# A new written order for the steps of both halves of a fused attention, gated MLP and rational MLP kernel

## The chip, the cores and the metric

The kernel runs on one core of one Trainium2 chip. The metric is the device time in microseconds (us) of one execution. Engines are named as in the profile: PE is TensorE (PEld its weight loads), DVE is VectorE, ACT is ScalarE, POOL is GpSimd, SP is SyncE, whose queue issues nearly all DMA transfers.

## What is computed

The reference, cut to what matters (8 batches, 8 heads, 576 rows of 64; 4608 tokens of 512):

```python
p_packed = sm_attn(p, k, v)            # 32 packed queries per head read the whole sequence
out = sm_attn(q, p_packed, p_packed)   # the sequence reads the 32 packed rows
x = out as (4608, 512)
xn = x / rms(x) * rms_g
x = (silu(xn @ w_gate) * (xn @ w_val)) @ w_out         # d_ff 1536
h = x @ w_in                                           # d_ff 2048
g = (a0 + a1 h + a2 h^2 + a3 h^3) / (1 + |b0||h| + |b1| h^2 + 1e-6)
return g @ w_out2
```

## The kernel before

Products that need float32 accuracy are done as three float16 products: each operand is split into a high part (written by ACT) and a low part (the difference, written by DVE or POOL). The weights arrive as 64-bit numbers and are decoded on DVE by three integer operations (lines 131, 135, 137).

**First half** (batches 0 to 7). For each batch attention gives normalised tokens (`an`, lines 655 to 919), and the packed values times the gate and value weights give `mt` (lines 415 to 447), so that the gated MLP needs only short products. The MLP is cut into two column ranges of 256 and 320 tokens and 12 blocks of 128 features. For each there are the steps G (gate product, line 1340), A (tanh on ACT, 1351), D (DVE, 1355), V (value product, 1340), E (DVE, 1358), Y and Z (high and low part of `y`, ACT 1362 and POOL 1367); the steps O and o are the second product (line 1393), P and S evict and store the result (`x2e`, 1372 and 1385). G, V, O and the attention's products take turns in five PSUM banks of the pool `ps_m`: a product can start only when the step that reads the bank's last content (D, E, P) is done. Meanwhile the weights of the third MLP are decoded, recombined and split (steps that begin with u, lines 1500 to 1534, POOL and ACT) and stored.

**Second half** (nine token blocks of 512, j = 0 to 8). The product with `w_in` is done with seven products instead of eight (a Strassen-like scheme). The operands `xo` of a block are made from the loaded block `xf` by the steps x: `s3` to `s6` sums on DVE (line 1636), `h0` to `h6` high parts on ACT (1626, 1630), `l0` to `l6` seven low parts on POOL (1633). A group g (block j, one of four column groups) has the products m1 to m7 (line 1685, `h`), the evictions k1 to k3 on ACT (`su`, 1693; products 6, 7 and 4 add to the bank that these read, so each of them must wait for the eviction ahead of it), sums a1 to a3 on DVE (1696), and for each of four result tiles the rational function: A (two ACT operations, 1726 and 1728), w and W (POOL, 1731 and 1736), t and u (DVE, 1739 and 1742), l and x (Ln and Exp on ACT, 1745 and 1748), q, e, g (DVE, 1751, 1754, 1757), h and i (high and low part of the result, ACT 1761 and POOL 1765). Then come the products o with `w_out2` (line 1789), the eviction f and the store F (1805, 1807, 1811). Products A, B and C of a group take turns in three PSUM banks of the pool `ps_h`; step g frees one.

**What sets the order.** Every step is a small function in the dictionary `steps`, and one long text, `ORDER` (line 947), names all 6932 of them in the order in which their instructions are put into the engines' queues. Each engine works its own queue strictly in that order and waits, where an operand is not there yet, with all that is queued behind. The text has four segments, parted by `|`, between which memory pools change: 3422 steps (the first half up to batch 7's MLP), 256 (the rest of batch 7, with the loads of the second half's weights), 82 (the first group of the second half) and 3172 (the rest). In the last segment the order repeats itself: the stretch from the first product of a block to the first product of the next has, from block 3 to block 6, the same 362 names in the same order, shifted by a block (block 2 nearly so, block 7 but for its end); blocks 0 and 1 are ordered freely.

```python
seg = [x.split() for x in ORDER.split("|")]
for nm in seg[0]:
    steps[nm]()
```

Of the kernel before, what the change touches and what calls it, by code (L numbers as in the profile page):

```python
# [9 lines left out]
F32 = mybir.dt.float32  # L10
# [27 lines left out]
def attention_pack_glu_rational_kernel(  # L38
# [641 lines left out]
    def attention(b):  # L680
# [1206 lines left out]
```

## Time and profile before

| what | value |
|---|---|
| time, median of 3 runs | 1498.63 us (1497.63 to 1499.5) |
| the profiled execution's own time | 1500.81 us |
| its span, first to last instruction | 1499.0 us |
| mean granted TensorE clock | 0.991 |
| PE busy | 1441.7 us, 96% of the span |
| DVE, ACT, POOL busy | 1197.8, 999.9, 858.8 us |
| DMA | 149.55 MB, mean 100 GB/s |

The span is what lies between the first and the last instruction; the profiled execution took 1.8 us more than its span and 2.2 us more than the median of the runs. Busy time is the sum of what an engine executed; a matmul's end is modelled, so PE's idle time is read as a lower bound of what it loses.

### The profile page before, as it was taken

The numbers are of one execution on the slowest core, as the hardware profiler recorded it, in microseconds if no ns is written. First come the engines' busy times: TensorE is split into PE (matmuls) and PEld (weight loads), VectorE is DVE, ScalarE is ACT, GpSimd is POOL, SyncE is SP. The second block draws the span as 40 slices with busy tenths as digits, with TensorE's granted clock in tenths as the row PEclk, the third lists the DMA queues.
The fourth block names the chain that finished last, engine by engine and source line by source line (L and its number), as shares of the span: only waits on it lengthen the run. The fifth ranks groups of instructions, "written<-read, shape, count | busy, mean of one in ns | idle before, by whom it ended". The sixth has DMA issues, their size and how long they took to land.

```text
span 1499.0 us, 31046 instructions
## 1 busy us (share of the span) xinstructions
PE 1441.7 (96%) x11940; PEld 1014.9 (68%) x11940; DVE 1197.8 (80%) x2160; ACT 999.9 (67%) x2042; POOL 858.8 (57%) x898
## 2 busy tenths in 40 slices
PE   7879999998999999999999999999999999999998
PEld 5557776867777677777877665666666666666665
DVE  5899867799887979987358897888787888787776
ACT  3555766776666676676357876777776767676665
POOL 1133142545557465353447877768686868686665
PEclk8899999999999999999999999999999999999999
DMA  9776663556868676795621001101010101000000
GB/s 269 196 223 134 127 148 69 108 138 145 190 158 203 153 193 165 199 193 131 255 94 34 29 15 43 57 1 57 1 57 1 57 1 57 1 15 15 15 15 29
DMA packets 212581, 149.55 MB, mean 100 GB/s; under 512 B 151888, under 2 KB 186704, under 8 KB 211280
## 3 DMA queue, kind: packets, MB, share of 16 engines
q1 hardware_dynamic: 212336, 147.57, 38.0%
q8 instruction: 93, 1.52, 0.4%
q14 instruction: 56, 0.46, 0.1%
q0 software_dynamic: 96, 0.01, 0.0%
HBM read 85.46 MB, written 30.41 MB: 77 GB/s over the span
## 4 chain that ended last, share of the span: by engine, by line
PE 67%; DVE 13%; POOL 9%; ACT 6%; issue 3%; DMA 2%; SPq 0%; ACTq 0%; DVEq 0%; POOLq 0%
PE o L1789 17%; PE h L1685 15%; PE o L1393 14%; PE gv L1340 13%; POOL xo L1633 2%; POOL w L1736 2%; POOL g L1765 2%; POOL w L1731 1%; PE xo L891 1%; DVE raw L135 1%; PE mm L415 1%; DVE t L1358 1%; PE mm L417 1%; PE pk L811 1%; DVE t L1355 1%
## 5 line engine op out<-in xcount | busy, mean ns | idle before, releaser
L1789 PE MATMUL o<-w2o,g 128*128 128x512 f16 x1728 | 410.6, 379 | 0.0
L1685 PE MATMUL h<-xo,w2t 128*128 128x256 f16 x3024 | 368.6, 272 | 9.8 <-ACT su L1693 9.6
L1685 PEld LDWEIGHTS <-w2t 128*128 128x128 f16 x3024 | 295.4, 98 | 97.9 <-issue 17.6
L1340 PE MATMUL gv<-an,mt 128*128 128x256 f16 (+1 forms) x2304 | 306.8, 286 | 14.7 <-DVE t L1355 6.4
L1393 PE MATMUL o<-y,wo 128*128 128x256 f16 (+1 forms) x2304 | 303.0, 287 | 6.6 <-DVE t L1355 3.3
L1367 POOL TENSOR_TENSOR y<-t,y 128x256 f16<-128x256 f32 (+1 forms) x192 | 161.9, 852 | 253.3 <-ACT y L1362 233.8
L1340 PEld LDWEIGHTS <-mt 128*128 128x128 f16 x2304 | 222.8, 98 | 79.3 <-issue 21.3
L1789 PEld LDWEIGHTS <-g 128*128 128x128 f16 x1728 | 169.0, 98 | 154.6 <-POOL g L1765 0.2
L1393 PEld LDWEIGHTS <-wo 128*128 128x128 f16 x2304 | 223.5, 98 | 73.9 <-issue 16.2
L1765 POOL TENSOR_TENSOR g<-t,g 128x512 f16<-128x512 f32 x140 | 167.8, 1199 | 115.4 <-ACT g L1761 115.4
L1736 POOL TENSOR_TENSOR w<-w,ah 128x512 f32<-128x512 f32 x140 | 178.7, 1278 | 10.8
L1731 POOL TENSOR_SCALAR w<-ah,cf 128x512 f32<-128x512 f32 x140 | 109.0, 779 | 58.1 <-ACT ah L1726 58.1
L1761 ACT ACTIVATE g<-t 128x512 f16<-128x512 f32 x140 | 88.5, 634 | 62.0 <-DVE t L1757 62.0
L1355 DVE SCALAR_TENSOR_TENSOR t<-t,gv 128x256 f32<-128x256 f32 (+1 forms) x192 | 84.5, 446 | 52.4 <-ACT t L1351 51.4
L1362 ACT ACTIVATE y<-t 128x256 f16<-128x256 f32 (+1 forms) x192 | 81.8, 437 | 62.6 <-DVE t L1358 61.4
L1351 ACT ACTIVATE t<-gv 128x256 f32<-128x256 f32 (+1 forms) x192 | 76.6, 405 | 70.4 <-PE gv L1340 51.1
L1745 ACT ACTIVATE h<-w,one 128x512 f32<-128x512 f32 x105 | 72.9, 695 | 69.7 <-POOL w L1736 51.6
L1751 DVE SCALAR_TENSOR_TENSOR t<-t,cf,h 128x512 f32<-128x512 f32 x105 | 78.1, 743 | 48.1 <-ACT h L1748 46.9
L1358 DVE SCALAR_TENSOR_TENSOR t<-t,gv 128x256 f32<-128x256 f32 (+1 forms) x192 | 84.5, 448 | 39.1 <-PE gv L1340 33.1
L1728 ACT ACTIVATE t<-h,cf 128x512 f32<-128x512 f32 x105 | 82.3, 783 | 0.8 <-POOL g L1765 0.8
L1742 DVE SCALAR_TENSOR_TENSOR t<-t,cf,h 128x512 f32<-128x512 f32 x105 | 78.4, 747 | 3.4
L1726 ACT ACTIVATE ah<-h 128x512 f32<-128x512 f32 x108 | 64.5, 597 | 22.1 <-PE h L1685 13.9
(223 smaller groups left out, 2161.0 us busy)
## 6 DMA issues: line engine op xcount, KB each, us to landing
raw<-in_moe_w_out_dram SPq DMA_DIRECT2D x28, 512.0 KB, 4.2
xf<-x2s SPq DMA_DIRECT2D x9, 1024.0 KB, 4.8
raw<-in_k_dram SPq DMA_DIRECT2D x16, 512.0 KB, 5.1
raw<-in_q_dram SPq DMA_DIRECT2D x16, 512.0 KB, 4.5
raw<-in_v_dram SPq DMA_DIRECT2D x16, 512.0 KB, 5.2
raw<-in_moe_w_in_dram SPq DMA_DIRECT2D x16, 512.0 KB, 4.6
out_dram<-osb SPq DMA_DIRECT2D x32, 256.0 KB, 2.4
w2t<-raw SPq DMA_DIRECT2D x28, 256.0 KB, 2.6
```

Of the source, the lines that this page charges most:

```text
L1340: nc.tensor.matmul(out=ps, lhsT=mt[b, nm, c // 4, g][:, l, cs], rhs=an[b][:, 2 * r_ + g, cols], start=(n == 0), stop=(n == 5))
L1355: stt(out=t, in0=t, scalar=1.0, in1=ps_g, op0=ALU.add, op1=ALU.mult)
L1358: stt(out=t, in0=t, scalar=S_Y / (2.0 * (S_AN * S_M) ** 2), in1=ps_v, op0=ALU.mult, op1=ALU.mult)
L1367: nc.gpsimd.tensor_tensor(out=y[:, 1], in0=t, in1=y[:, 0], op=ALU.subtract)
L1393: nc.tensor.matmul(out=ps, lhsT=wo1[c][:, l, d * 128:(d + 1) * 128], rhs=ys[b, h, c][:, r_, :], start=(c == 0 and n == 0), stop=(c == NF1 ...
L1685: nc.tensor.matmul(out=st[x][:, W2 * e:W2 * e + W2], lhsT=w[:, l, 128 * cs:128 * cs + 128], rhs=xs[j][:, OPERAND[p], r_, kc], start=(first ...
L1728: act(out=st["t", n], in_=st[x], func=AF.Identity, scale=cf[:, 0:1], bias=cf[:, 7:8])
L1731: nc.gpsimd.tensor_scalar(out=st["w", n], in0=st["ah", n], scalar1=cf[:, 6:7], scalar2=cf[:, 5:6], op0=ALU.mult, op1=ALU.add)
L1736: nc.gpsimd.tensor_tensor(out=st["w", n], in0=st["w", n], in1=st["ah", n], op=ALU.mult)
L1761: act(out=g[:, 0], in_=st["t", n], func=AF.Copy)
L1765: nc.gpsimd.tensor_tensor(out=g[:, 1], in0=st["t", n], in1=g[:, 0], op=ALU.subtract)
L1789: nc.tensor.matmul(out=po[k], lhsT=g[:, l, 256 * i + 128 * u:256 * i + 128 * u + 128], rhs=w2t["o", 0, c][:, r_, :], start=(done[k] == 0), ...
```

## The change

Only the text `ORDER` is new. Each of its four segments names the same steps as before, each once; the second and the third segment are word for word the same (only their line breaks differ), the first and the last are in another order throughout. No instruction is added, removed or resized. The text is one line longer, so that every line below it has a number higher by one.

```diff
     ORDER = (
-        "wl9 wb9 0pl 0pf 0ph L1 0kf10 0kf12 0kg10 0kg12 wl7 wc9 wd9 0kf11 0kg11 0am1 cc L0 0kf00 wb7 0kg00 0kf01 "
+        "L1 0kf10 wl4 wb4 wc4 wd4 0pl 0kf12 0pf 0ph 0kf11 0kg10 wl2 0kg12 wb2 wc2 wd2 cd 0kg11 0am1 L0 0kf00 wl3 "
...
```

In the last segment the repeated pattern is gone: the order differs from block to block throughout.

**Second half, POOL, while the operands of block 4 are made.** `xo` rows are the low parts of the block's operands (from `xf`, the loaded block, or `sx`, a sum of its quarters), `w` rows the two steps of the rational function's denominator, `g` rows the low parts of its result. Before:

```order
L1633 TENSOR_TENSOR xo<-xf,xo 128x512
L1765 TENSOR_TENSOR g<-t,g 128x512
L1633 TENSOR_TENSOR xo<-sx,xo 128x512
L1731 TENSOR_SCALAR w<-ah,cf 128x512
L1736 TENSOR_TENSOR w<-w,ah 128x512
L1765 TENSOR_TENSOR g<-t,g 128x512
L1633 TENSOR_TENSOR xo<-xf,xo 128x512 x2
L1731 TENSOR_SCALAR w<-ah,cf 128x512
L1736 TENSOR_TENSOR w<-w,ah 128x512
L1765 TENSOR_TENSOR g<-t,g 128x512
L1633 TENSOR_TENSOR xo<-xf,xo 128x512
L1633 TENSOR_TENSOR xo<-sx,xo 128x512
```

Now, from the first of this block's `xo` rows on:

```order
L1634 TENSOR_TENSOR xo<-sx,xo 128x512
L1766 TENSOR_TENSOR g<-t,g 128x512
L1634 TENSOR_TENSOR xo<-xf,xo 128x512
L1732 TENSOR_SCALAR w<-ah,cf 128x512
L1766 TENSOR_TENSOR g<-t,g 128x512
L1732 TENSOR_SCALAR w<-ah,cf 128x512
L1737 TENSOR_TENSOR w<-w,ah 128x512 x2
L1732 TENSOR_SCALAR w<-ah,cf 128x512
L1737 TENSOR_TENSOR w<-w,ah 128x512
L1766 TENSOR_TENSOR g<-t,g 128x512
L1732 TENSOR_SCALAR w<-ah,cf 128x512
L1737 TENSOR_TENSOR w<-w,ah 128x512
```

All seven `xo` operations of a block stood within 13 rows of POOL's queue (six of them are shown); now they stand within 33 rows for block 4, two in the first twelve. For block 8, the last, they stand within 18 rows.

**Opening, SP's queue from the program's first transfer on.** `raw` and `rawt` are k or q of batch 0, `praw` is p, numbered `raw_` tiles are weights. Before:

```order
L148 DMA raw_178<-in_moe_w_gate_dram 128x512
L293 DMA praw<-in_p_dram 32x8x64
L251 DMA raw<-in_k_dram 128x4x256
L255 DMA rawt<-in_k_dram 64x4x64
L148 DMA raw_211<-in_moe_w_val_dram 128x512
L251 DMA raw<-in_k_dram 128x4x256
```

Now:

```order
L251 DMA raw<-in_k_dram 128x4x256
L255 DMA rawt<-in_k_dram 64x4x64
L148 DMA raw_191<-in_moe_w_val_dram 128x512
L293 DMA praw<-in_p_dram 32x8x64
L148 DMA raw_221<-in_moe_w_gate_dram 128x512
L251 DMA raw<-in_k_dram 128x4x256
```

The first load of k is the first transfer now and was the third; p is the fourth and was the second; the second load of k is the sixth in both. PE's queue begins with the transposes of k (line 490) now, and began with those of p (line 473).

## Rows read from the trace of the kernel before

**Rows 1.** The page's parts 1 and 2: PE's busy time, and its granted clock.

```profile
PE 1441.7 (96%) x11940; PEld 1014.9 (68%) x11940; DVE 1197.8 (80%) x2160; ACT 999.9 (67%) x2042; POOL 858.8 (57%) x898
PEclk8899999999999999999999999999999999999999
```

**Rows 2.** Windows by stage: length; busy PE, PEld, DVE, ACT, POOL; PEclk, DMA share, GB/s.

```profile
0.00:112.00 112.00, 86.96 (x702) 58.84 (x703) 88.50 (x197) 54.63 (x132) 21.05 (x35) 0.89 0.80 229
112.00:340.00 228.00, 225.12 (x2288) 167.96 (x2286) 182.51 (x408) 150.15 (x362) 86.55 (x120) 1.00 0.56 123
340.00:600.00 260.00, 245.22 (x2551) 187.34 (x2539) 220.47 (x436) 173.06 (x418) 151.97 (x167) 1.00 0.72 171
600.00:768.00 168.00, 167.30 (x1593) 129.41 (x1592) 111.57 (x243) 94.36 (x231) 69.66 (x86) 1.00 0.70 191
799.00:922.00 123.00, 122.95 (x821) 79.84 (x820) 109.33 (x159) 92.18 (x158) 99.63 (x91) 1.00 0.08 27
922.00:1443.00 521.00, 511.35 (x3437) 335.80 (x3435) 424.89 (x630) 377.01 (x646) 379.88 (x353) 1.00 0.07 25
1443.00:1499.00 56.00, 51.85 (x322) 31.15 (x319) 39.83 (x61) 34.44 (x58) 33.03 (x31) 0.98 0.05 20
```

**Rows 3.** Waits of PE from 922 to 1443: us in total, times, longest.

```profile
PE h L1685 <- ACT su L1693: 9.6, 12, 1.3
```

**Rows 4.** Timeline of PE around 1025: start, us, [idle before <- releaser].

```profile
1025.26 1.47 PE L1685 MATMUL h<-xo,w2t 128*128 128x256 f16 x12 [1.29 <-ACT su L1693]
1031.04 1.47 PE L1685 MATMUL h<-xo,w2t 128*128 128x256 f16 x12 [0.41 <-ACT su L1693]
```

**Rows 5.** Timeline of POOL just before that.

```profile
1022.12 1.16 POOL L1633 TENSOR_TENSOR xo<-xf,xo 128x512 f16<-128x512 f32 x1
1023.24 1.16 POOL L1633 TENSOR_TENSOR xo<-sx,xo 128x512 f16<-128x512 f32 x1
1024.38 0.77 POOL L1731 TENSOR_SCALAR w<-ah,cf 128x512 f32<-128x512 f32 x1
```

**Rows 6.** Timeline of ACT in the same stretch.

```profile
1021.08 0.69 ACT L1745 ACTIVATE hd<-w,one 128x512 f32<-128x512 f32 x1 [1.09 <-POOL w L1736]
1024.58 0.62 ACT L1693 ACTIVATE su<-h 128x512 f32<-128x512 f32 x1
```

**Rows 7.** Waits of weight loads from 799 to 1443.

```profile
PEld L1685 <- DVE t L1757: 1.3, 3, 0.5
```

**Rows 8.** Timeline of SP, then of PE, in the first 8 us.

```profile
0.72 0.39 SPq L148 DMA_DIRECT2D raw<-in_moe_w_gate_dram  x1
1.64 0.45 SPq L251 DMA_DIRECT2D raw<-in_k_dram  x1
...
5.32 0.60 PE L473 MATMUL first<-squares,praw 32*128 32x32 f32 x4 [5.32 <-DMA praw<-in_p_dram]
6.93 1.33 PE L490 MATMUL first<-squares,raw 128*64 128x128 f32 x10 [1.01 <-DMA raw<-in_k_dram]
```

**Rows 9.** Two windows of the opening, columns as in rows 2.

```profile
12.15:29.20 17.05, 13.60 (x189) 10.39 (x186) 14.29 (x39) 9.26 (x25) 0.00 (x0) 1.00 1.04 320
29.20:49.70 20.50, 18.93 (x106) 13.55 (x113) 14.42 (x30) 5.96 (x14) 0.00 (x0) 0.50 0.75 220
```

**Rows 10.** Waits of PE from 340 to 600, the largest.

```profile
PE gv L1340 <- DVE t L1355: 5.5, 5, 1.9
```

**Rows 11.** Timeline of DVE and of POOL from 348 to 353.

```profile
348.68 1.48 DVE L749 SCALAR_TENSOR_TENSOR v<-rawt,v 64x256 f16<-64x256 f32 x1
351.17 1.36 DVE L749 SCALAR_TENSOR_TENSOR x16in<-raw,x16in 128x256 f16<-128x256 f32 x1
...
348.41 1.48 POOL L1534 TENSOR_TENSOR raw<-raw,raw 128x512 f32<-128x512 f32 x1 [0.27 <-ACT raw L1500]
```

**Rows 12.** Instructions of two lines: duration ns min/median/max, first and last start us, forms.

```profile
L749 DVE SCALAR_TENSOR_TENSOR v<-rawt,v x14: 403/409/1480, 130.5 to 662.4; 64x256 f16<-64x256 f32 x14
L1355 DVE SCALAR_TENSOR_TENSOR t<-t,gv x192: 400/424/489, 57.3 to 767.0; 128x256 f32<-128x256 f32 x96, 128x320 f32<-128x320 f32 x96
```

761 rows, old and new, of the table ORDER are left out of this document.

## The prediction

> **What bounds the kernel now.** I read the page first, for which engine is full; then the windows by stage, for where that engine loses time; then the waits of each stage and the timeline around one of them. PE is busy for 1441.7 of 1499.0 us [rows 1]. Since no instruction is added or removed, an order can win only what PE does not use, 57.3 us, and what it does at the lower clock; both must be looked for by stage. The windows [rows 2] are to be read as length minus PE busy. The first 112 us lose 25.0 us; 112 to 340 loses 2.9; 340 to 600 loses 14.8; 600 to 768 loses 0.7. In the second half, 799 to 922 loses 0.05 us in 123, 922 to 1443 loses 9.65 in 521, and the end loses 4.1. So there are three places: the opening, the middle of the first half, and the repeated part of the second half.
>
> The repeated part has one cause. All of PE's waits there are products that wait for an eviction by ACT: 12 waits, 9.6 us [rows 3], two for each of six blocks, of some 1.3 and 0.4 us [rows 4]. The timeline shows why. POOL makes the seven low parts of the next block's operands, 1.16 us each and so 8.1 us, in one run of 13 queue rows [rows 5]; with them it has no pause and falls behind with the denominators (w, then W). ACT works strictly in order, and its Ln step stands there waiting for W, 1.09 us at 1021 [rows 6]. The eviction is queued behind that Ln and starts at 1024.58; PE's product follows at 1025.26 [rows 4]. The stretch from 799 to 922, whose order is not the repeated one, has the same mix of work and loses nothing.
>
> **The change, part by part.** The sum is made against the profiled execution, 1500.81 us; the median of the runs is 2.2 us lower, and the result is carried to it at the end.
>
> *The second half.* The seven low parts of block 4 now lie within 33 rows of POOL's queue, where they lay within 13; for block 8 they lie within 18. The other blocks from 2 on are like block 4: counted in the written order, their seven span 48 to 82 us of PE's products, where it was 13.6 us from block 3 on. Upper bound of the gain: all 12 waits, 9.6 us. What a free order costs by itself: 0.05 us in 123 [rows 2], so 0.2 in 521. One block of six, block 8, is still crowded and may keep its 1.7 us; I charge half, 0.85. Term: 9.6 - 0.2 - 0.85, about 8.5 us gained. What the moved steps pass: SP's queue, where the block loads stand among the output stores; in the new text each of them comes after stores whose evictions stand well ahead of it, so I cost that at nothing. The cover is that the operands have tens of us of products ahead of them; without it a block load (1 MB) would show in full.
>
> The other bound of this term comes from the PSUM banks. Of the 105 products that open a bank of the three, 4 stood, before, directly behind the DVE step that frees the bank, with no product between; now 26 do. The four showed as three waits of the weight load, 1.3 us in all, 0.43 each [rows 7], and PE itself lost none of it in its window. So between 0 and 26 x 0.43 = 11.2 us are to be set against the gain. I take the end near 0, since the window that holds those hand-offs lost 0.05 us.
>
> *The opening.* PE waits 5.32 us for p and 1.01 more for k [rows 8]. The load of k moves from the third place in SP's queue to the first, so its issue comes 0.92 us earlier (1.64 - 0.72), and PE's first work is on k. Behind it stands a chain of attention steps in which nothing is long enough to hide anything, so I let it through: 1 us gained. The bounds are wide, since the rest of the opening is shuffled too and the clock sits on it: from 29.2 to 49.7 us the granted clock is 0.50, the 1.2 GHz level, with PE busy for 18.9 of 20.5 us, after a stretch at 1.00 in which it was busy for 13.6 of 17.05 us [rows 9]. If the new order keeps the upper level, 2.4 GHz, there, up to 9.5 us go (half of 18.9); if a second such stretch appears, as much comes.
>
> *The middle of the first half.* Of the 14.8 us that PE loses from 340 to 600, the largest part is products that wait for a bank that DVE has not yet read [rows 10]. DVE is late there for a reason that the order only sets by chance: some of its operations are stretched. At 348.68 one that takes 0.40 at least took 1.48, and at 351.17 another took 1.36, while POOL was in a 1.48 us operation that began at 348.41 [rows 11]. Of 14 alike the longest took 1480 ns and the median 409; the 192 that read a product from PSUM stay between 400 and 489 [rows 12]. The new order moves both sides of such meetings. The number of tight places is the same: of the first half's 538 takings of a bank, 118 followed the freeing step by 0.7 us of products or less, now 113. So I scale the loss of the two middle windows, 14.8 + 2.9, by 113/118 and gain 0.8 us; the bounds are all of the 14.8 gone and as much again lost.
>
> The Trainium skill has a rule for the stretch (SBUF — State Buffer, section "Who interferes with whom"): a DVE instruction with two inputs in SBUF and a GpSimd instruction that reads SBUF shut each other out, and the second to issue blocks until the first is done. The rows agree: the stretched ones read two SBUF tiles, the 192 that never stretch read PSUM. By that rule durations measured under one order are not those of another, and a plan made with them can meet new collisions; this is the third rival.
>
> *Sum.* 8.5 + 1 + 0.8 = 10.3 us. The profiled execution would take 1490.5, and the median **1488 us** (1498.63 - 10.3, rounded), 0.7% faster. From no change a measurement of this kernel tells some 0.2%, 3 us.
>
> **The rivals.**
>
> *First: the first half gains as well.* The opening keeps the upper clock (9.5 us) and half of the stalls from 340 to 600 go (7.4): with the second half's 8.5 this gives 1498.6 - 25.4 = 1473 us. For it speaks that 39.8 us lie idle in these two stretches, against it that DVE is busy for 88.5 of the first 112 us [rows 2] with decoding that the order cannot remove, and that the tight places are as many as before.
>
> *Second: the bank hand-offs cost what the weight loads showed.* Place: the products that open a bank in the second half. 26 x 0.43 = 11.2 us against 8.5 gained in that half: with the 1.8 of the first half the time is 1498.6 - 8.5 + 11.2 - 1.8, 1499.5 us, no change. It decides once a hand-off costs PE more than 0.33 us. Against it: the window from 799 to 922.
>
> *Third, on the other side: collisions of DVE and POOL in the first half.* Place: 340 to 600, where POOL is busy for 152 of 260 us [rows 2] and each stretched DVE step holds a bank of five. If they take as much again, 14.8 us, the time is 1498.6 - 8.5 - 1 + 14.8, **1504 us**. It decides from a first-half loss of 9.5 us more than now. For it speaks that the losses there are few and large, 1.1 us in the mean and up to 1.9 [rows 10], so that nine more are enough; against it that the loads of DVE and POOL ahead of each product are within some 6 us of what they were all along the first half, by the order and the mean durations of the lines.
>
> **How the numbers follow.** I give the forecast 0.60, with 1480 to 1496 us as its own range (first-half terms up to 8 us either way); the first rival 0.15; the second 0.12; the third 0.13. Faster by over 0.2%, below 1495.6: nearly all of the forecast, the first rival, and a sixth of the second, 0.77. Within 0.2%: the rest of the second, 0.10. Slower by over 0.2%: the third, 0.13. The range leaves out the outer part of the first and of the third rival: 1472 to 1502 us.
>
> **What would show it.** Right: from some 920 us on PE busy fills its windows to within 0.1 us in 40, the waits of products for `su` fall from 9.6 to under 2.5 us, and those that remain lie where block 8's operands are made. The first matmul works on k and starts about 6 us after the span's start. From 340 to 600 PE loses 10 to 20 us, at other places than now, each behind a DVE operation longer than 1 us. Wrong: weight loads waiting for L1758 (the old 1757) twenty times or more (second rival); PE losing over 25 us between 340 and 600 (third); a granted clock of 0.50 in other stretches of the opening than 29 to 50 us; or, in the second half, new waits of PE for the low parts of results or for a block load, which I cost at nothing.

## The result and the profile after

The changed kernel takes **1473.29 us** (median of 4 runs, 1472.64 to 1476.24) against 1499.07 for the kernel before on the same chip (4 runs): the ratio is 0.9828, 95% interval 0.9805 to 0.9851. That is 25.8 us faster where 10.3 were forecast. The direction and the range held; the size is wrong by more than a factor of two.

From the page of the changed kernel. Its lines answer to [rows 1]; the line numbers below the order's text are higher by one. The last line shows the weight loads of the second half's products.

```profile
PE 1433.8 (97%) x11940; PEld 1016.3 (69%) x11940; DVE 1181.4 (80%) x2160; ACT 998.3 (68%) x2042; POOL 846.9 (58%) x898
PEclk9889999999999999999999999999999999999999
L1686 PEld LDWEIGHTS <-w2t 128*128 128x128 f16 x3024 | 295.8, 98 | 80.1 <-issue 0.4
```

The windows by stage of the changed kernel, columns as in [rows 2]:

```profile
0.00:112.00 112.00, 86.83 (x707) 58.74 (x708) 89.03 (x201) 57.18 (x137) 23.41 (x35) 0.88 0.78 228
112.00:340.00 228.00, 226.65 (x2292) 171.72 (x2291) 184.01 (x414) 153.30 (x369) 86.39 (x123) 1.00 0.60 128
340.00:600.00 260.00, 252.89 (x2662) 193.08 (x2660) 221.34 (x453) 174.99 (x424) 146.56 (x167) 1.00 0.74 180
787.00:922.00 135.00, 135.00 (x947) 92.57 (x946) 121.75 (x185) 111.16 (x192) 111.95 (x105) 1.00 0.07 25
922.00:1440.00 518.00, 518.00 (x3493) 341.59 (x3491) 436.09 (x649) 383.67 (x658) 386.13 (x362) 1.00 0.08 25
```

Length less PE busy, before and after: the opening loses 25.0 and 25.2 us, 112 to 340 loses 2.9 and 1.35, 340 to 600 loses 14.8 and 7.1, and the repeated part of the second half 9.65 and 0.00. The first product of the second half starts at 767.9 before and at 754.6 now. So of the 26.9 us between the two spans (1499.0 and 1472.1) 13.3 are won in the first half and 13.6 in the second. Of the 13.3, by the time from the start of each product to the start of the next from 130 us on, 8.7 lie at the gate and value products (L1340 before) and 2.7 at those of the packed values (L417).

Three measures recur below, worked out from all records of a trace. **Loss by start to start**: from the start of each product of the second half to the start of the next, less what it takes where nothing waits (0.109 us for 256 columns, 0.216 for 512), summed from 800 to 1430 us where it is over 0.03. It is 13.4 us in 33 places before and 0.0 now. **Denominators late behind a low part**: the first steps `w` of POOL from 922 to 1443 that start more than 0.15 us after their input `ah` is there, with a low part of the next block's operands directly ahead of them in POOL's queue. **Work done** by a time: the products that PE has started, each counted with the median time to the next start that its line and shapes have in the kernel before. Where two orders differ in it, one is ahead by so much; PE's busy time does not tell that: in the first 112 us the kernel before is busy for 87.0 us at a mean granted clock of 0.89 and does 72.7 us of work, second_half_only for 87.9 us at 0.82 and does 68.6. By this measure the changed kernel is ahead by 0.8 us at 130 us, 3.6 at 340, 11.0 at 600 and 13.3 at 740.

### The profile page after: what moved, and what is told of

Read it like the earlier page. It is cut to its first block, busy times and chain, and to the rows that moved or that the text cites. A ratio compares the mean times of both kernels' runs of the same rounds, so it can differ in the third digit from the quotient of the medians.

```text
span 1472.1 us, 31080 instructions
## 1 busy us (share of the span) xinstructions
PE 1433.8 (97%) x11940; PEld 1016.3 (69%) x11940; DVE 1181.4 (80%) x2160; ACT 998.3 (68%) x2042; POOL 846.9 (58%) x898
## 4 chain that ended last, share of the span: by engine, by line
PE 85%; DVE 9%; ACT 2%; DMA 2%; issue 1%; POOL 1%; SPq 0%; ACTq 0%; DVEq 0%; POOLq 0%
PE o L1790 25%; PE h L1686 22%; PE gv L1341 16%; PE o L1394 14%; PE xo L891 1%; PE mm L417 1%; PE pk L811 1%; PE s L857 1%; DVE raw L135 1%; DVE t L1359 1%; PE mm L415 1%; DVE t L1356 1%; DVE v L749 1%; DVE raw L137 1%; DVE n L911 1%
## 5 line engine op out<-in xcount | busy, mean ns | idle before, releaser
L1368 POOL TENSOR_TENSOR y<-t,y 128x256 f16<-128x256 f32 (+1 forms) x192 | 150.8, 792 | 241.0 <-ACT y L1363 224.9
L1394 PEld LDWEIGHTS <-wo 128*128 128x128 f16 x2304 | 224.4, 98 | 70.2 <-issue 11.3
L1766 POOL TENSOR_TENSOR g<-t,g 128x512 f16<-128x512 f32 x140 | 162.6, 1168 | 62.7 <-ACT g L1762 56.0
L1752 DVE SCALAR_TENSOR_TENSOR t<-t,cf,h 128x512 f32<-128x512 f32 x105 | 78.0, 743 | 23.5 <-ACT h L1749 22.4
L1694 ACT ACTIVATE su<-h 128x512 f32<-128x512 f32 x108 | 64.2, 595 | 37.3 <-PE h L1686 28.9
L1740 DVE TENSOR_TENSOR t<-t,h 128x512 f32<-128x512 f32 x105 | 71.6, 682 | 19.3 <-ACT t L1729 18.3
```

What stands on the lines that cost most here:

```text
L1368: nc.gpsimd.tensor_tensor(out=y[:, 1], in0=t, in1=y[:, 0], op=ALU.subtract)
L1394: nc.tensor.matmul(out=ps, lhsT=wo1[c][:, l, d * 128:(d + 1) * 128], rhs=ys[b, h, c][:, r_, :], start=(c == 0 and n == 0), stop=(c == NF1 ...
L1766: nc.gpsimd.tensor_tensor(out=g[:, 1], in0=st["t", n], in1=g[:, 0], op=ALU.subtract)
```

## The experiments

### The two halves apart

The four segments of the text can be exchanged, as each names the same steps in both kernels.

```diff
 first_half_only:  first segment new, last segment old
 second_half_only: first segment old, last segment new
```

> The new order in the first segment only, the old one in the last. Theory A (from the two traces: the first product of the second half starts 13.3 us earlier in the changed kernel, and the second half loses 13.7 us less, and the two have nothing to do with each other): 1499.1 - 13.3 = 1486 us, within 3; the first product of the second half at about 755 us; from then on the old picture, some 12 waits of products for su, about 9.6 us. Theory B (the gain of one half hangs on the order of the other, for instance because the seam or the block loads fit only together): more than 1490 us.

> The old order in the first segment, the new one in the last. Theory A (the halves are independent): 1499.1 - 13.7 = 1485 us, within 3; the first product of the second half at about 768 us as before; no wait of a product for su from 922 to 1443. Theory B (as above): more than 1490 us. If the forecast's own upper bound for this half had been right (all 12 waits listed, 9.6 us), 1489.5.

Measured: 1486.99 us, ratio 0.9910 (0.9893 to 0.9928), and 1487.38 us, ratio 0.9914 (0.9893 to 0.9935). The product of the two is 0.9825, the whole change 0.9828: theory A, the halves have nothing to do with each other. With the old last segment the old waits are there, the same row as [rows 3] but for 0.1 us; with the new one there is no wait of PE from 922 to 1443. The waits of PE there in first_half_only:

```profile
PE h L1685 <- ACT su L1693: 9.5, 12, 1.3
```

### Second half: is it the spread, the evictions or the lead?

**spread_operands** takes the forecast at its word: the old order, with only the operands' steps (on DVE, ACT and POOL) and the block loads behind them spread.

```diff
-g30m60 x4h0 g23i1 ... g30m61 ... x4h3 g30m70 g23q2 x4h5 g30m71 x4l3 g23e2 g23l3 g23o000 g30k3 g23g2 x4l0 ...
+g30m60 g23i1 ... x4h0 g30m70 g23q2 g30m71 g23e2 ... x4h3 ... x4h5 ... x4l3 g30m21 ... g30h0 x4l0 g30a2 ...
```

> The old order, with one thing changed: the 17 steps that make the operands of each of blocks 3 to 8, and the load of the next block behind them, are spread over 260 rows of the last segment where they stood in some 110. Theory A (POOL's run of seven low parts is the cause of the second half's loss: it makes the denominators late, Ln late, and the evictions behind Ln late): the waits of products for su from 922 to 1443 fall from 9.6 us to under 1.5, and 12 to 13 us go, as in the changed kernel's second half: 1486 to 1488 us. Theory B (the loss comes from the periodic order as such, in which each eviction stands close ahead of its product): at least 6 us of these waits stay and the time is over 1492.

Measured: 1505.16 us, ratio 1.0029 (1.0014 to 1.0044). **Theory A as I had put it falls**: with each low part far from the next, the kernel is slower than before, the loss 17.0 us. The waits of PE from 900 to 1450, then POOL, ACT and PE around one of them:

```profile
PE h L1685 <- ACT su L1693: 11.5, 18, 1.8
```

```profile
1045.90 1.16 POOL L1633 TENSOR_TENSOR xo<-xf,xo 128x512 f16<-128x512 f32 x1
...
1049.13 1.15 POOL L1633 TENSOR_TENSOR xo<-xf,xo 128x512 f16<-128x512 f32 x1
1050.25 1.15 POOL L1765 TENSOR_TENSOR g<-t,g 128x512 f16<-128x512 f32 x1
1051.39 0.76 POOL L1731 TENSOR_SCALAR w<-ah,cf 128x512 f32<-128x512 f32 x1
...
1047.15 0.61 ACT L1726 ACTIVATE ah<-h 128x512 f32<-128x512 f32 x1
...
1053.54 0.69 ACT L1745 ACTIVATE h<-w,one 128x512 f32<-128x512 f32 x1 [1.53 <-POOL w L1736]
1054.17 0.58 ACT L1693 ACTIVATE su<-h 128x512 f32<-128x512 f32 x1
...
1054.80 1.47 PE L1685 MATMUL h<-xo,w2t 128*128 128x256 f16 x12 [0.47 <-ACT su L1693]
```

The input `ah` is there at 1047.76 (1047.15 + 0.61). POOL finishes another denominator, works on one low part and on a result's low part, takes this denominator at 1051.39, and Ln stands 1.53 us. The block's previous low part began 3.2 us earlier and its next one comes 7.4 us later: seven together are not needed. There are 23 denominators late behind a low part here, 18 before.

**no_low_parts** leaves the low parts out.

```diff
         def lo(n, src):
-            nc.gpsimd.tensor_tensor(out=flat(n, 1), in0=src(), in1=flat(n, 0), op=ALU.subtract)
+            return
...
-                        rhs=xs[j][:, OPERAND[p], r_, kc], start=(first and e == 0 and n == 0), stop=(n == 5), skip_group_check=True,
+                        rhs=xs[j][:, OPERAND[p], 0, kc], start=(first and e == 0 and n == 0), stop=(n == 5), skip_group_check=True,
```

> The old order; the seven low parts of each block's operands are left out on POOL in the second half, and the products that would read them read the high parts a second time, so PE's work is the same. Theory A (POOL's low parts are what makes the denominators, the Ln and then the evictions late, and each one ahead of a denominator costs something, which is why spreading them won nothing): the waits for su vanish (under 0.5 us), the loss from 922 to 1443 falls from 13.1 us, by start to start, to under 2: 1486 to 1488 us. Theory L alone (the lead of 1.13 us is too short whatever POOL does): half or more of the waits stay: over 1492.

Measured: 1489.04 us, ratio 0.9926 (0.9909 to 0.9942). No wait of PE is listed, and the loss is 1.3 us in 19 places: 12.1 of the 13.4 us come through POOL's low parts. The time itself is just above the 1486 to 1488 expected. PE's window from 922 to 1443 is full:

```profile
922.00:1443.00 521.00, 521.00 (x3516) 343.69 (x3514) 426.49 (x644) 387.50 (x661) 343.14 (x319) 1.00 0.08 25
```

**evictions_ahead**, **evictions_ahead_2** and **evictions_ahead_all** leave the low parts bunched and move ACT's evictions directly behind the product that they evict: in the first group of blocks 3 to 8, in the second group of blocks 2 to 7, in every group of blocks 2 to 8. In the second group (the first variant moves `k2` and `k3` alone):

```diff
-g41m10 g40e1 x5l6 x6L g40A3 g41m11 g40g1 g40w2 g33o300 g40t2 g41k1 g33o310 ... g41m61 g40i1 g40l2 g40u3 g33o301 g41k2 ...
+g41m10 g40e1 x5l6 x6L g41m11 g41k1 g40A3 g40g1 g40w2 g33o300 g40t2 g33o310 ... g41m61 g41k2 g40i1 g40l2 g40u3 g33o301 ...
```

> The old order, with one thing changed: the two evictions k2 and k3 of the first group of each of blocks 3 to 8 stand directly behind the product that they evict, and so ahead of the Ln step in ACT's queue; the operands' steps stay bunched. Theory A (the eviction is late only because ACT stands in an Ln that waits for POOL): the waits for su fall under 2 us and 9 to 13 us go: 1486 to 1490 us, as POOL's lateness has nobody else that it reaches. Rival C (POOL's lateness reaches PE by another way as soon as this one is closed: the Ln is later still, then exp, the result g, and the products o that read it): the waits for su go, but products wait at least 4 us for g, its low part or a bank, and the time is over 1493.

> The old order; the waits of before lie in the second group of a block, not in its first, so now the three evictions k1, k2, k3 of the second group of blocks 2 to 7 stand directly behind the product that they evict: k1 ahead of the step A3 (two ACT operations), k2 and k3 ahead of a Ln. The operands' steps stay bunched. Theory A (the evictions are late because of what stands ahead of them in ACT's queue): k1 can start 1.14 us earlier, at the end of the Abs that ran from 1022.30, and k3 0.6 earlier, so of the 2.02 us lost per block 0.3 to 0.5 stay; 9 to 10 us go over six blocks: 1490 us. Rival C (the lateness of POOL's denominators reaches PE by another way: A3 and Ln are later still, then the results g and the banks): new waits of products for g or for a bank, and less than 4 us gained: over 1496.

> The old order with the low parts bunched as they were; the evictions k1, k2, k3 of every group of blocks 2 to 8 stand directly behind the product that they evict, k1 ahead of the previous group's step A3, k2 and k3 ahead of a Ln. In evictions_ahead_2, where only the second group of a block had this, a wait of 0.8 us passed to the third group's k1, which stood behind A3. Theory E (the place of the evictions in ACT's queue decides): the waits for su fall under 1 us and the loss from 922 to 1443 under 2: 1486 to 1489 us. Theory A alone (POOL's lateness has to be paid by PE somewhere): waits for su or for banks of 4 us or more stay: over 1492.

Measured: 1500.27 us, ratio 0.9996 (0.9985 to 1.0008); 1494.56 us, ratio 0.9961 (0.9946 to 0.9976); 1495.63 us, ratio 0.9967 (0.9956 to 0.9979). The first tells nothing: I had put it into the wrong group, since the waits lie in the second one, and its 12 waits are all there (10.5 us). The other two win about 5 us each and leave a loss of 8.4 us, in kind as rival C has it: the wait passes on. PE's waits from 922 to 1443 in evictions_ahead_2, then the next group of the same block there:

```profile
PE h L1685 <- ACT su L1693: 4.8, 6, 1.1
```

```profile
1039.59 0.59 ACT L1726 ACTIVATE ah<-h 128x512 f32<-128x512 f32 x1
1040.06 0.78 ACT L1728 ACTIVATE t<-h,cf 128x512 f32<-128x512 f32 x1
1040.72 0.61 ACT L1726 ACTIVATE ah<-h 128x512 f32<-128x512 f32 x1
1041.20 0.80 ACT L1728 ACTIVATE t<-h,cf 128x512 f32<-128x512 f32 x1
1041.86 0.62 ACT L1693 ACTIVATE su<-h 128x512 f32<-128x512 f32 x1
...
1042.54 1.47 PE L1685 MATMUL h<-xo,w2t 128*128 128x256 f16 x12 [0.79 <-ACT su L1693]
```

ACT is in no Ln here; it works without a pause and the eviction is still late, behind two pairs of steps that came late themselves. And in evictions_ahead_all, where every eviction is written directly behind its product, 11 waits of at most 0.6 us stay; in the six of 0.6 us ACT still works without a pause on a pair ahead of the eviction (from 1020.74 to the eviction's start at 1021.88). So theory E gets a part of the loss (5.0 of 13.4 us) and theory A the rest: POOL's lateness stays in the chain until PE has paid for it.

**longer_lead** puts two more products between the filling of a bank and the product that needs it evicted.

```diff
-g41m11 g40g1 g40w2 g33o300 g40t2 g41k1 g33o310 ... g41m60 ... g41m61 ... g33o301 ... g33o311 ...
+g41m11 g40g1 g40w2 g33o300 g40t2 g41k1 g33o310 ... g33o301 ... g33o311 ... g41m60 ... g41m61 ...
```

> The old order; in the second group of blocks 2 to 7 four output products stand between the first product of bank A and the one that needs the bank evicted, where two stood (in the trace 1.13 us from the end of the one to the start of the other, without a wait); the group's later products come two places later. Operands bunched, ACT's order as it was. Theory L (what the changed order does in the second half is to lengthen this lead: its median is 2.43 us there, and 1.13 in each of the 84 places before): the waits for su fall from 9.6 us to under 1.5 and 11 to 13 us go: 1487 to 1489 us. Rival D (the periodic order is a closed loop of three banks: what is gained at this lead is lost at the next opening of a bank, which now stands nearer behind the step that frees it): waits of products or of weight loads for the freeing steps appear, and less than 5 us are gained.

Measured: 1498.51 us, ratio 0.9994 (0.9981 to 1.0008); loss 11.3 us in 33 places. Neither theory has it right. The lead without a wait grows from 1.13 to 2.43 us and the product starts 2.55 us behind the filling one, so the wait at `k1` is all but gone; the wait for a bank that rival D expects does not appear. But the waits for evictions move on, to `k3` and to the next group's `k1`. PE's waits from 922 to 1443:

```profile
PE h L1685 <- ACT su L1693: 7.1, 11, 0.9
```

**bunched_operands** and **bunched_low_new** go the other way, in the new order: all operand steps of blocks 3 to 8 close together, and only five of POOL's low parts close together.

```diff
 bunched_low_new, block 4: x4l1, x4l2, x4l5, x4l0, x4l4 taken from five places over 205 steps
-... x4s6
+x4l1 ... x4l2 ... x4l5 ... x4l0 ... x4l4 ... x4s6
```

> The new order in both halves, with one thing changed in the last segment: the steps that make the operands of each of blocks 3 to 8 stand as close together as in the old order (all seven low parts within 15 to 18 steps of POOL's queue, where they lay within 37 to 56 for blocks 3 to 7), just ahead of the block's first product. Theory S (what removes the waits is the new order's slack: from the end of an eviction to the next product on its bank 1.04 us in the median, against 0.08 in the old order; where the low parts lie matters little): no wait of a product for su above 1 us in all, and the time within 3 us of the new order, 1471 to 1476. Theory A (bunched low parts make POOL late by some 8 us and the evictions with it): about 2 us for each of six blocks come back: 1480 to 1486.

> The new order in both halves; in the last segment five of the seven low parts of each of blocks 3 to 8 (all whose place is free) are brought together on POOL, within 6 to 11 of its steps where they lay within 13 to 52; nothing else moves. Theory A (low parts in a run make POOL's denominators late, and with them Ln and the evictions behind it): five of them hold POOL up by 5.8 us, waits of products for su or for a bank come back in each block, 1 to 2 us each: 1479 to 1485 us. Theory S (the new order's slack, 1.04 us in the median behind an eviction, takes up what the low parts do): waits under 1.5 us in all, 1472 to 1476.

Measured: 1497.71 us, ratio to the kernel before 0.9989 (0.9975 to 1.0003), loss 25.1 us; and 1488.17 us, ratio 0.9934 (0.9911 to 0.9956), loss 13.0 us in 9 places. Theory S falls: the new order's slack does not take up low parts in a wrong place, and moving five of them in six blocks brings back 13.0 us, about all that the second half had won. The first of the two costs still more, but it moves ACT's and DVE's steps too, and POOL stands 10.7 us waiting for high parts, so it shows less. PE's waits from 760 to 1450 in bunched_low_new, then POOL, ACT and PE at one of them:

```profile
PE h L1686 <- DVE t L1758: 5.8, 4, 2.1
PE h L1686 <- POOL xo L1634: 2.8, 1, 2.8
PE h L1686 <- ACT su L1694: 2.6, 2, 1.7
```

```profile
1036.63 1.15 POOL L1634 TENSOR_TENSOR xo<-xf,xo 128x512 f16<-128x512 f32 x1
1037.75 1.15 POOL L1634 TENSOR_TENSOR xo<-sx,xo 128x512 f16<-128x512 f32 x1
1038.89 1.30 POOL L1732 TENSOR_SCALAR w<-ah,cf 128x512 f32<-128x512 f32 x1
1040.17 1.15 POOL L1766 TENSOR_TENSOR g<-t,g 128x512 f16<-128x512 f32 x1
...
1041.35 0.78 ACT L1729 ACTIVATE t<-h,cf 128x512 f32<-128x512 f32 x1 [3.39 <-POOL g L1766]
...
1046.50 0.71 PE L1686 MATMUL h<-xo,w2t 128*128 128x256 f16 x5 [1.53 <-DVE t L1758]
```

One of the three waits is of another kind: 2.8 us at one product that waits for a low part itself, which my move had put too late. The other 8.4 follow late denominators by some 4 to 15 us, but only the 2.6 for `su` end as the waits of before did. In the rows shown the low parts also hold up a result's low part (1040.17); ACT stands 3.39 us until that is done, and the DVE step that frees PE's bank is late.

What the new order does with a low part shows in its own trace, POOL first and then ACT:

```profile
985.41 1.15 POOL L1634 TENSOR_TENSOR xo<-xf,xo 128x512 f16<-128x512 f32 x1
986.70 0.77 POOL L1732 TENSOR_SCALAR w<-ah,cf 128x512 f32<-128x512 f32 x1
...
985.99 0.60 ACT L1727 ACTIVATE ah<-hd 128x512 f32<-128x512 f32 x1
```

The low part ends at 986.56, and the denominator's input at 986.59: the 1.15 us lie in a gap that POOL had anyway. The count over the stage:

| kernel | denominators late behind a low part, us together | loss by start to start, us |
|---|---|---|
| before | 18 of 104, 23.4 | 13.4 |
| spread_operands | 23 of 103, 18.4 | 17.0 |
| longer_lead | 18 of 104, 23.4 | 11.3 |
| evictions_ahead_all | 18 of 105, 23.3 | 8.4 |
| no_low_parts | 0 of 106 | 1.3 |
| changed kernel | 2 of 107, 4.9 | 0.0 |
| second_half_only | 3 of 107, 5.4 | 0.0 |
| bunched_low_new | 8 of 104, 29.2 | 13.0 |
| bunched_operands | 13 of 101, 29.4 | 25.1 |

The last 1.3 us and the late ones that cost nothing point at a second difference, which no run changes alone. In blocks 2 to 8 there are 84 evictions of this kind. Before, the next product on the bank starts 0.08 us after the eviction's end in the median, and 59 of the 84 leave it less than 0.1; in the changed kernel the median is 1.04 us, and one leaves it less than 0.1.

### First half

**no_y_low_old** and **no_y_low_new** take POOL's 192 low parts out of the first half.

```diff
     def y_lo(b, h, c, t):
         y = ys[b, h, c]
-        nc.gpsimd.tensor_tensor(out=y[:, 1], in0=t, in1=y[:, 0], op=ALU.subtract)
+        return
...
-                rhs=ys[b, h, c][:, r_, :],
+                rhs=ys[b, h, c][:, 0, :],
```

> The old order; in the first half the 192 low parts of the gated product (POOL, about 0.85 us each) are left out and the output products read the high part in their place, so PE's work is the same. In the trace of the old order 137 DVE operations of the first half last over 0.15 us longer than the shortest of their form, 73.5 us in all, and 77 of them, 36.8 us, lie beside such a low part. Theory K (PE's losses from 112 to 768 us, 18.4 us in gaps, come from DVE operations stretched beside POOL): the stretch falls to about 37 us, and the loss to under 9, so 8 to 11 us go: 1489 to 1492. Rival M (the losses come from where the order puts the DVE steps; the stretch is harmless): less than 4 us gained.

> The new order, with the same low parts left out. In its trace 100 DVE operations of the first half are stretched, 57.6 us in all, 48 of them, 22.4 us, beside such a low part; PE loses 8.9 us in gaps from 112 to 760. Theory K: the stretch falls to about 35 us and 3 to 5 us go: 1468 to 1470 us; with the old order's 8 to 11 the distance between the two orders in the first half shrinks from 13.3 us to about 8 or less, which is what their unequal stretch is worth. Rival M: under 2 us gained here, and the distance between the two stays at 13.

Measured: 1482.59 us, ratio 0.9887 (0.9872 to 0.9901), and 1463.24 us, ratio to the kernel before 0.9763 (0.9739 to 0.9787). Stretched is a DVE operation over 0.15 us longer than the shortest of its line and shapes in the trace, in the first 780 us (how forms are told apart moves the counts by a few; the expectations count 137 and 100):

| kernel | stretched operations, us | PE's gaps from 112 us to the second half, us | first product of the second half, us |
|---|---|---|---|
| before | 136, 73.0 | 18.4 | 767.9 |
| changed | 97, 56.5 | 8.9 | 754.6 |
| no_y_low_old | 53, 31.0 | 4.9 | 749.8 |
| no_y_low_new | 50, 32.0 | 3.1 | 743.8 |

Theory K, and by more than it expected: the old order wins 18.1 us to the second half's first product, the new one 10.8, and the distance between the two shrinks from 13.3 to 6.0 us once their stretch is alike. The windows from 340 to 600, old order first:

```profile
340.00:600.00 260.00, 255.85 (x2683) 197.05 (x2682) 210.69 (x462) 179.12 (x435) 93.09 (x96) 1.00 0.79 184
...
340.00:600.00 260.00, 256.91 (x2693) 198.27 (x2689) 216.00 (x459) 179.08 (x439) 93.30 (x98) 1.00 0.77 187
```

Of the remaining 6.0 us 3.6 lie in the opening: by the work done no_y_low_new is ahead by 3.6 us at 130 us, 4.4 at 340, 5.1 at 600 and 6.1 at 740. So from 130 to 740 us the distance is 12.5 us with the low parts and 2.5 without them. The runs leave out POOL's time as well as the meetings with DVE, so they bound what the meetings cost and do not isolate it. What speaks for the meetings is the trace of before: of its 14 gaps of PE over 0.5 us from 112 to 770, 13 come after 8 us in which 1.3 to 4.0 us of stretch fell on DVE, and in the 6 us ahead of each DVE had at most 0.9 us of idle time; of all whole microseconds in that stretch 21% meet both conditions. The waits of the changed kernel from 340 to 600, the largest, to be read against [rows 10]:

```profile
PE o L1394 <- DVE mt L431: 1.6, 1, 1.6
PE s1a L770 <- DVE pT L704: 1.1, 1, 1.1
...
PE gv L1341 <- DVE t L1356: 0.7, 1, 0.7
```

**old_opening** grafts the old order's first 400 steps onto the rest of the new first segment.

```diff
 first segment: steps 1 to 400 in the old order, all others in the new one; last segment old
```

> The first 400 steps in the old order (to about 117 us), the rest of the first segment in the new order, the last segment in the old one. To be compared with the new first segment whole (1487.0 us). Theory E (the opening's new order is worth nothing or at most the 1 us forecast; the first half's gain comes from 340 us on): 1486 to 1489. Rival F (the first half's gain hangs on where the opening leaves the engines): over 1491.

Measured: 1497.22 us, ratio 0.9984 (0.9971 to 0.9997). That is in rival F's range, but it does not answer the question: the seam made a wait of its own, at 136.7 us.

```profile
PE gv L1340 <- DVE t L1355: 3.3, 1, 3.3
```

By the work done it lies behind first_half_only by 1.6 us at 130 us, 5.9 at 340, and no more than 6.4 at 740; from 340 to 600 it loses as little as the new order (87.60, 87.81 and 78.20 us busy in windows of 90, 90 and 80). What the opening brings is seen better without a graft. In the eight profiles with the old first segment and the first half's low parts the work done at 130 us is 85.0 to 89.4 us, 87.7 in the median; in the four with the new one it is 87.4 to 89.7, 89.1 in the median. So it may bring some 1.4 us, less than profiles of one order differ.

## Why the prediction was right or wrong

**Right: where the time could come from.** Nothing but idle PE time could be won, and it was won in the second half's repeated part and in the middle of the first half. The opening's 1 us can be neither shown nor excluded: the first matmul works on k and starts at 4.83 us, the work done at 130 us is 0.8 us ahead. The wait for `su`, the chain over POOL's `w` and ACT's Ln, and the low parts as its origin are borne out by no_low_parts. Bank hand-offs cost nothing, as assumed: weight loads wait 0.4 us in all from 760 to 1440, so the second rival falls. Block 8's low parts, within 18 steps, cost nothing either, where I had charged 0.85 us. Two of the signs failed. PE loses 7.1 us from 340 to 600, not 10 to 20, and a granted clock of 0.50 came in other stretches of the opening too (49.5 to 56.3 and 87.1 to 93.8 us), which left its mean over the first 112 us at 0.88, where it was 0.89.

**Wrong, the second half's term: "Upper bound of the gain: all 12 waits, 9.6 us."** It was no upper bound; 13.6 us went. The idle time of a row understates what a wait costs. PE of the kernel before around the first wait of [rows 4]:

```profile
1022.51 1.46 PE L1789 MATMUL o<-w2o,g 128*128 128x512 f16 x6
1025.26 1.47 PE L1685 MATMUL h<-xo,w2t 128*128 128x256 f16 x12 [1.29 <-ACT su L1693]
1026.56 1.46 PE L1789 MATMUL o<-w2o,g 128*128 128x512 f16 x6
```

Six products of 512 columns take 1.30 us when nothing waits (6 x 0.216), but here the next group starts 2.75 us later: 1.45 lost, 1.29 listed. The twelve waits cost 11.6 us for 9.6. Beside them 21 delays, nearly all of some 0.08 us, 1.8 us in all, are in no row, since the modelled end of a matmul covers them.

**Wrong, the reason behind that term: "their seven span 48 to 82 us of PE's products, where it was 13.6 us".** I took the spread itself for the cure. spread_operands shows that it is none, and bunched_low_new that the places matter all the same: the new order puts nearly every low part where no denominator is ready, and leaves a microsecond behind each eviction. The distance from one low part to the next says neither. It was also counted wrong ahead of the forecast: block 4's low parts stand within 54 rows of POOL's queue (51 where equal neighbours are one row), not within 33.

**Wrong, the first half's term: "So I scale the loss of the two middle windows, 14.8 + 2.9, by 113/118".** The number of tight places stayed and the loss halved. The term was 0.8 us, and from 130 to 740 us 12.5 came, which this step could not have given: the stalls come where DVE is stretched and has no time in hand, and the stretch itself fell from 73.0 to 56.5 us. How much of the 12.5 the meetings cost alone stays open, since the runs that show it take POOL's work away with them. The first rival had half of these stalls gone (7.4 us; 340 to 600 gave 7.7), and its time, 1473 us, is what was measured; but the 9.5 us that it took from the opening came instead from the second half, from the other windows of the first, and from losses that no row lists. Its time was met by a wrong sum. The third rival had the same mechanism with the other sign.

The rule of the Trainium skill (SBUF — State Buffer, section "Who interferes with whom") by which that rival went says what a meeting does and not whether a new order has more of them: this one has 97 stretched operations for 136. My reading that the stretched ones read two SBUF tiles was true of the rows shown alone; 31 of the 136 read one.

## What to carry to other kernels

Size what waiting costs from the start of one product to the start of the next, not from the listed idle time; here the latter left out over a quarter. When a helper engine's extra work makes a strict queue late, ask of each piece whether what stands behind it is ready at that moment. Here 0 to 3 such pieces went with a loss of 0 to 1.3 us and 8 to 23 with one of 8 us or more; the distance between the pieces did not tell these kernels apart. And in an order without slack, curing one wait passes it to the next group, so an order repaired at one place has to be priced over the whole loop.

## What was not expected of the hardware

DVE is stretched not only where it reads two SBUF tiles. The first decoding step reads one tile (423 ns in the median) and took 1.26 us, all but the last 0.3 beside a POOL operation that only writes; in the changed kernel two operations that read two tiles took 0.42 us each, their usual time, beside the same kind of POOL operation. DVE and POOL of the kernel before, then of the changed one:

```profile
114.90 1.26 DVE L131 TENSOR_SCALAR raw<-raw 128x512 int32<-128x512 int32 x1
...
114.90 0.99 POOL L1563 MEMSET pkz<- 128x512 f16 x2
```

```profile
131.02 0.42 DVE L749 SCALAR_TENSOR_TENSOR v<-raw,v 128x256 f16<-128x256 f32 x1
131.35 0.42 DVE L749 SCALAR_TENSOR_TENSOR x16in<-raw,x16in 128x256 f16<-128x256 f32 x1
...
130.54 0.98 POOL L1564 MEMSET pkz<- 128x512 f16 x2
```

The Trainium skill (same page and section) tells the two cases apart in this way: a DVE operation with two SBUF inputs contends with a POOL operation that reads SBUF and not with one that only writes, while a one-input operation contends when it runs in a mode that takes both ports. The rows agree with the first; that the decoding step runs in such a mode no run here shows, though its 423 ns against the 693 of the two-tile step L135 of the same size would fit it.

The opening's granted clock is not set by the order alone. With the same first segment, the stretch from 85 to 104 us had the upper level, 2.4 GHz, throughout in the kernel before (1.00) and fell below it for a part in second_half_only (0.91 in the mean), where PE was busier:

```profile
85.00:104.00 19.00, 13.04 (x101) 8.07 (x100) 18.65 (x40) 10.73 (x26) 6.29 (x7) 1.00 0.77 196
```

```profile
85.00:104.00 19.00, 14.26 (x113) 8.50 (x113) 18.03 (x40) 11.74 (x31) 7.17 (x9) 0.91 0.66 178
```

Differences of 2 us in the opening are therefore below what one profile of each order can tell; the work done at 130 us differs by 4.4 us among the eight profiles of the old order.
